# A two-branch kernel (spectral filter and softmax attention) whose instruction order is planned with a lock between GpSimd and VectorE

## The chip, the cores and the metric

The kernel runs on one core of a Trainium2 chip. A core has five engines with queues of their own: TensorE (PE; PEld is its weight load), VectorE (DVE), ScalarE (ACT), GpSimd (POOL) and SyncE (SP), which issues most DMAs. Each engine takes its instructions strictly in the order of its queue and waits on semaphores where one needs another engine's result. The metric is the device time of one execution in microseconds (us); less is better. In the rows below, arena is the one large on-chip buffer and ps the eight banks of the accumulator memory.

## The reference

Two independent branches are computed and laid side by side in the output, 640 columns each:

```python
def _A_ref(x, w_r, w_i):            # x: (1, 2048, 640)
    X = rfft2(x.astype(float32))    # over both axes
    X = X * (w_r + 1j * w_i)
    return irfft2(X, s=(2048, 640)).astype(bfloat16)

def _B_ref(x, wqkv, wo):            # x: (1, 2048, 640), 32 heads of 20
    qkv = (x @ wqkv).reshape(1, 2048, 3, 32, 20).transpose(2, 0, 3, 1, 4)
    q, k, v = qkv[0], qkv[1], qkv[2]
    p = softmax(einsum("bhqd,bhkd->bhqk", q, k) * 20 ** -0.5)
    o = einsum("bhqk,bhkd->bhqd", p, v)
    return o.transpose(0, 2, 1, 3).reshape(1, 2048, 640) @ wo

out = concatenate([_A_ref(...), _B_ref(...)], axis=-1)
```

## The kernel before

**Branch B, attention.** x is transposed on TensorE (job `xT`, L598), multiplied by the weights into keys and queries (jobs `p01` for keys and `p00` for queries of the first head groups, L620; `pk` for the others, L649) and into values (job `V`, L698). The first weights have to be copied apart first (`padw`, a VectorE copy, L559). A unit of work is four heads times 512 queries; there are 32 units of 64 score tiles of 128 keys by 512 queries, 2048 tiles in all. A tile's scores are one matmul (L817). Its exponential is taken in one of two ways:

- on ScalarE, two tiles in one instruction (`exp`, L1444, 128x1024);
- on VectorE, four tiles as a batch: the score is clipped into 16-bit integers (`p1`, L972, from ps), and two further 16-bit passes over 128x2048 elements in the arena make two more terms (`p2` L1020 and `p3` L1019). A batch multiplies the values three times, so it needs three times the matmuls L1102 of a ScalarE tile, and a scaled copy of the values (`vs`: GpSimd L1029, or VectorE L1031 early on).

TensorE multiplies values by the exponentials (`pv`, L1102); at the end of a unit the sum goes out of ps (L1133), its reciprocal takes a round trip through DRAM, and GpSimd scales the result (`onorm`, L1154). Job `OP` (L1248 and L1253) is the last projection, evicted at L1259 and stored.

**Branch A, the filter.** GpSimd folds x by its symmetries (`fold`, L1659 to L1666); jobs S1 (L1772), S2 (L1855), S3 (L1959) and S4 (L2011) are matmuls by tables with VectorE work behind each (S2: L1887 and L1895 to L1904; S4: a copy L2019 for a first half, and two L2030 for a second half). S4 is 32 jobs of six matmuls, four jobs for each of eight row blocks; a block is stored when its four jobs are done, and the second half of block n waits until block n-2 has been stored.

**What sets the order.** No order is written by hand. While the kernel is built, the class `KB` plays the whole program through with a clock of its own (`now`, and `free[engine]` for when each engine is done). At each step `step_pe` takes for TensorE, in this order: scores for ScalarE if two banks are free, multiplications by values, background jobs (`try_bg`, by priority `prio`, and only if the time left until ScalarE needs scores again has room for them), scores for VectorE (`try_dve_fill`). `pick_dve` takes for VectorE the ready instruction with the lowest priority number, and `pick_dve_tile` with `dve_wants` decides from VectorE's planned backlog how many tiles VectorE gets; ScalarE gets the rest. `put` books an instruction with an assumed duration and moves the planned clocks. So a changed duration or rule in the planner changes nothing that is computed, but can change every queue's order and the split of the 2048 tiles. On the chip the instructions then follow the queues and the semaphores.

Before, `put` knew one interaction between GpSimd and VectorE: a `p2` or `p3` that begins while GpSimd is busy was booked as longer by 0.44 of the overlap.

## Time and profile before

| | before |
|---|---|
| timed runs, us | 756.99, 756.69, 755.43 (median 756.69) |
| span of the profiled execution, us | 759.9 |
| that execution outside its span | no time of its own is given beside the span |
| ScalarE busy, us | 723.8 (95%), of it 774 exponentials 716.6 |
| TensorE busy, us | 722.7 (95%) |
| VectorE busy, us | 678.2 (89%) |
| GpSimd busy, us | 206.7 (27%) |
| granted TensorE clock, mean | 0.994 |

Busy shares are averages over the whole program. Matmuls are pipelined, and a matmul's record is longer than the time until the next can start, so TensorE's 95% is not a limit by itself; idle time before an instruction, and what ended it, says who waited for whom.

### The profile page before, as it was taken

How to read it: one execution, taken by the hardware profiler on the slowest of the kernel's cores; microseconds unless marked ns; L12 is line 12 of the kernel's file. 1: busy time of each engine (PE TensorE's matmuls, PEld its weight loads, DVE VectorE, ACT ScalarE, POOL GpSimd, SP SyncE). 2: the span in 40 equal slices, each digit the busy share in tenths (PEclk: the TensorE clock that was granted, in tenths of full speed). 3: DMA queues.
4: the chain of work that ended last, by engine and by line, in shares of the span. 5: the costliest groups of instructions: out<-in, count | busy, mean ns of one | idle time of the engine just before them, and what ended most of it. 6: DMA issues, size and time to landing. Idle time of an engine off the chain costs nothing.

```text
span 759.9 us, 16458 instructions
## 1 busy us (share of the span) xinstructions
PE 722.7 (95%) x6520; PEld 232.3 (31%) x6565; DVE 678.2 (89%) x1172; ACT 723.8 (95%) x787; POOL 206.7 (27%) x253
## 2 busy tenths in 40 slices
PE   8998999999999999999999999999999999999997
PEld 4422232332322222232223323322222232333333
DVE  3599999989989899999989988999899999999895
ACT  5899999999999999999999989999999999999994
POOL 7296952111211022122331123212121222122110
PEclk9999999999999999999999989999999999999999
DMA  9023321202102116213120112103010012111101
GB/s 314 11 72 90 96 71 52 48 20 49 34 21 57 42 46 222 76 37 104 38 53 16 47 37 51 24 21 110 20 44 22 16 46 84 38 45 48 51 23 56
DMA packets 43503, 44.68 MB, mean 59 GB/s; under 512 B 16740, under 2 KB 36582, under 8 KB 43166
## 3 DMA queue, kind: packets, MB, share of 16 engines
q1 hardware_dynamic: 42654, 42.25, 18.9%
q0 software_dynamic: 768, 1.32, 0.7%
q8 instruction: 54, 0.88, 0.5%
q14 instruction: 27, 0.22, 0.1%
HBM read 28.47 MB, written 8.36 MB: 48 GB/s over the span
## 4 chain that ended last, share of the span: by engine, by line
PE 51%; ACT 38%; DVE 9%; issue 2%; DVEq 0%
ACT arena L1444 37%; PE ps L817 18%; PE ps L1102 14%; PE ps L649 5%; DVE arena L972 3%; PE ps L698 3%; PE ps L1855 3%; PE ps L1772 2%; DVE arena L1019 2%; PE ps L1248 2%; PE ps L2011 2%; PE ps L1959 2%; DVE arena L1020 1%; PE ps L620 1%; PE ps L578 1%
## 5 line engine op out<-in xcount | busy, mean ns | idle before, releaser
L1444 ACT ACTIVATE arena<-ps 128x1024 f16<-128x1024 f32 x774 | 716.6, 1092 | 17.6 <-PE ps L817 11.2
L972 DVE TENSOR_SCALAR arena<-ps 128x512 int16<-128x512 f32 (+1 forms) x490 | 330.8, 692 | 31.8 <-PE ps L817 30.4
L817 PE MATMUL ps<-arena 32*128 32x512 bf16 x2048 | 304.9, 386 | 13.6 <-ACT arena L1444 10.0
L1102 PE MATMUL ps<-arena 128*32 128x512 f16 x3048 | 240.9, 386 | 4.4 <-DVE arena L1019 2.1
L817 PEld LDWEIGHTS ps<-arena 32*128 32x128 bf16 x2048 | 75.1, 91 | 285.9 <-ACT arena L1444 255.9
L1029 POOL TENSOR_SCALAR arena<-arena 128x96 bf16<-128x96 bf16 x112 | 74.5, 669 | 250.6 <-PE ps L1102 245.7
L1019 DVE TENSOR_SCALAR arena<-arena 128x2048 int16<-128x2048 int16 x125 | 93.7, 750 | 5.5 <-PE ps L1102 5.1
L1154 POOL TENSOR_TENSOR arena<-arena 128x512 bf16<-128x512 f32 x30 | 40.6, 1353 | 204.8 <-DMA arena<-rd 204.7
L1020 DVE TENSOR_SCALAR arena<-arena 128x2048 int16<-128x2048 int16 x125 | 92.9, 743 | 1.5
L1102 PEld LDWEIGHTS ps<-arena 128*32 128x32 bf16 x3048 | 52.3, 94 | 104.2 <-issue 70.2
L649 PE MATMUL ps<-arena 128*128 128x512 bf16 x149 | 45.7, 383 | 4.2 <-issue 2.4
L1855 PE MATMUL ps<-arena 128*128 128x322 bf16 (+1 forms) x198 | 39.2, 311 | 3.3 <-DVE arena L1904 1.8
L2011 PE MATMUL ps<-arena 128*128 128x320 bf16 (+1 forms) x192 | 35.7, 302 | 0.1
L698 PE MATMUL ps<-arena 128*128 128x160 bf16 x320 | 32.2, 234 | 1.0 <-DVE arena L972 1.0
L1887 DVE TENSOR_TENSOR arena<-ps,arena 128x644 bf16<-128x644 f32 (+1 forms) x34 | 27.9, 821 | 4.1 <-PE ps L1855 2.3
L1959 PE MATMUL ps<-arena 128*128 128x512 bf16 (+3 forms) x123 | 29.9, 333 | 1.3 <-issue 1.3
L1248 PE MATMUL ps<-arena 128*128 128x320 bf16 (+1 forms) x152 | 28.2, 302 | 0.2 <-DVE arena L1887 0.2
L1133 DVE COPY arena<-ps 128x512 f32<-128x512 f32 (+1 forms) x33 | 22.0, 669 | 5.9 <-PE ps L1102 5.6
L698 PEld LDWEIGHTS ps<-arena 128*128 128x128 bf16 x320 | 21.1, 98 | 14.7 <-issue 11.1
L661 DVE TENSOR_SCALAR arena<-ps 128x512 bf16<-128x512 f32 x34 | 23.1, 678 | 0.1
L1772 PE MATMUL ps<-arena 128*128 128x512 bf16 x72 | 21.7, 383 | 1.0 <-issue 0.8
L1855 PEld LDWEIGHTS ps<-arena 128*128 128x128 bf16 (+1 forms) x198 | 14.9, 98 | 21.6 <-issue 10.8
(83 smaller groups left out, 369.9 us busy)
## 6 DMA issues: line engine op xcount, KB each, us to landing
arena<-rd SPq DMA_DIRECT2D x120, 64.0 KB
out_dram<-arena SPq DMA_DIRECT2D x32, 160.0 KB
arena<-in_A_x_dram SPq DMA_DIRECT2D x16, 160.0 KB
xs<-arena SPq DMA_DIRECT2D x16, 160.0 KB
arena<-xs SPq DMA_DIRECT2D x4, 640.0 KB
arena<-arena SPq DMA_DIRECT2D x105, 20.0 KB
arena<-ct SPq DMA_DIRECT2D x2, 1024.0 KB
arena<-ct SPq DMA_DIRECT2D x4, 512.0 KB
```

The costliest lines, as they stand in the source:

```text
L649: return lambda e: e.matmul(o, l, r_, start=(cc == 0), stop=(cc == 4))
L698: return lambda e: e.matmul(o, l, r_, start=st, stop=(c == 4), skip_group_check=True)
L817: return e.matmul(self.ps[:, bank, :], self.KT[32 * j:32 * j + 32, g, kt * 128:(kt + 1) * 128], self.QT[32 * j:32 * j + 32, g, qc * 512:(q ...
L972: return e.tensor_scalar(o, in_, 0.0, 31744.0, ALU.max, ALU.min)
L1019: self.dve_push([(lambda e, en: e.tensor_scalar(Ii, Ii, SH2, 0.0, ALU.subtract, ALU.max), occ, ik + pk, ik, [], "p3")], lambda: push(self. ...
L1020: ops = [(lambda e, en: e.tensor_scalar(Gi, Ii, SH1, 0.0, ALU.subtract, ALU.max), occ, ik, [("G", b)], [], "p2")]
L1029: self.pool_op(lambda e: e.tensor_scalar(vs, vi, W1, None, ALU.mult), 300.0, r=vr, w=vk, name="vs")
L1102: inst = e.matmul(self.ps[32 * j:32 * j + 32, bank, :], v_, p_, start=s_, stop=False, tile_position=(0, 32 * j), skip_group_check=True)
L1444: self.put("act", lambda e: e.activation(o, in_, AF.Exp, bias=ACT_BIAS, scale=ACT_SCALE), 0.8333 * 512 * n + 60.0, r=[("ps", b) for b in b ...
L1855: return lambda e: e.matmul(o, lhs, r_, start=st, stop=sp)
L1959: return lambda bank: (lambda e: e.matmul(ps[0:M, bank, lo_:hi_], l, rhs, start=st, stop=sp, skip_group_check=True))
L2011: return lambda e: e.matmul(o, l, r_, start=(n == 0), stop=(n == 5))
```

## The change

The planner's model is changed in five ways; no instruction computes anything else than before.

- The lengthening by 0.44 of the overlap goes. In its place the names in `PORT` exclude one another between VectorE and GpSimd: such an instruction is booked to begin only when the other engine's last one of `PORT` is over (`plock`). `PORT` has the 16-bit passes `p2` and `p3`, `vs`, the weight copies `padw`, the second and later instructions of S2's eviction (renamed `S2.evL`), and nearly all that GpSimd does, its memsets too.
- `pick_dve` passes over an instruction of `PORT` while GpSimd's lock lasts more than 100 ns longer, and takes another one.
- The assumed times of GpSimd's work change (`onorm` 1600 to 1250 ns, `vs` 300 to 430, the folds).
- `p2` and `p3` are assumed 32 ns shorter for a batch, and `exp` 8 ns shorter.

```diff
+        self.plock = {"pool": 0.0, "dve": 0.0}
...
-        if eng == "dve" and name in ("p2", "p3", "p4") and self.free["pool"] > st:
-            occ += min(self.free["pool"] - st, 1.8 * occ) * 0.44
+        port = name in self.PORT
+        if port and eng == "dve":
+            st = max(st, self.plock["pool"])
+        if port and eng == "pool":
+            st = max(st, self.plock["dve"])
         end = st + occ
+        if port:
+            self.plock[eng] = end
...
+    PORT = {"p2", "p3", "vs", "S2.evL", "padw", "onorm", "fold", "ms_vp", "ms_v1", "ms_k", "ms_q", "x24z", "wpad", "wz", "ms_sb"}
...
-        occ = 100 + 0.26 * 512 * n
+        occ = 68 + 0.26 * 512 * n
...
-                ops.append((mk(J.bank), occ, [key] + list(rk), list(wk), list(pwk), J.name + ".ev"))
+                ops.append((mk(J.bank), occ, [key] + list(rk), list(wk), list(pwk), J.name + (".evL" if J.name == "S2" and ops else ".ev")))
...
             if self.P.peek(en, r=op[2], w=op[3], pw=op[4]) > self.now:
+                continue
+            if op[5] in self.PORT and self.plock["pool"] > self.now + 100.0:
                 continue
...
-        return 0.8333 * 512 * n + 60.0
+        return 0.8333 * 512 * n + 52.0
```

What this does to the queues is seen at three places. Lines of the changed kernel are 8 higher than those of before in branch B and 10 higher from L1444 on.

**The start.** TensorE's queue before, from its first matmul: 11 warm-up matmuls, 20 transposes, one filler, the first keys and queries (10 matmuls), 20 transposes, and then the first scores (L817).

```order
L578 MATMUL ps<-arena 128x512 x11
L598 MATMUL ps<-arena 128x128 x20
L1536 MATMUL ps<-arena 128x512
L620 MATMUL ps<-arena 128x512 x10
L598 MATMUL ps<-arena 128x128 x20
L817 MATMUL ps<-arena 128x512 x4
L698 MATMUL ps<-arena 128x160 x14
```

The same place in the changed kernel (scores are L825 now, the weight products L628).

```order
L586 MATMUL ps<-arena 128x512 x11
L606 MATMUL ps<-arena 128x128 x20
L628 MATMUL ps<-arena 128x512 x5
L606 MATMUL ps<-arena 128x128 x20
L628 MATMUL ps<-arena 128x512 x5
L706 MATMUL ps<-arena 128x160 x10
L628 MATMUL ps<-arena 128x512 x5
L606 MATMUL ps<-arena 128x128 x10
L825 MATMUL ps<-arena 128x512 x4
L706 MATMUL ps<-arena 128x160 x18
```

The first queries, which the first scores need, are now the third group of five, behind a second block of keys and ten value matmuls; the filler is gone. On VectorE, the four copies of weights (L559 before, L567 now) stood together at the head of the queue. In the changed kernel's VectorE queue they are spread:

```order
L567 COPY arena<-arena 128x20x20
L612 COPY arena<-ps 128x2x256 x2
L636 TENSOR_SCALAR arena<-ps,arena 128x512
L612 COPY arena<-ps 128x2x256
L612 COPY arena<-ps 128x3x256
L567 COPY arena<-arena 128x20x20
L636 TENSOR_SCALAR arena<-ps,arena 128x512
L567 COPY arena<-arena 128x20x20
L636 TENSOR_SCALAR arena<-ps,arena 128x512
```

The second copy, which the first queries need, stands behind four evictions of transposes (L612) and one of keys (L636).

**ScalarE.** The piece of the difference that holds its exponentials:

```order
-L604 COPY arena<-ps 128x3x256
-L604 COPY arena<-ps 128x2x256
-L604 COPY arena<-ps 128x3x256 x2
-L604 COPY arena<-ps 128x2x256
-L1444 ACTIVATE arena<-ps 128x1024 x774
+L612 COPY arena<-ps 128x3x256 x3
+L612 COPY arena<-ps 128x2x256
+L712 CAST arena<-ps 128x2x8x20
+L612 COPY arena<-ps 128x3x256
+L1454 ACTIVATE arena<-ps 128x1024 x780
```

Six exponentials more, so twelve tiles more are ScalarE's; VectorE has 122 batches in place of 125.

**The end.** TensorE's last rows of the main program before; the matmuls of S4 (L2011) ended among the scores, 32 rows ahead of the last one here.

```order
L1300 MATMUL ps<-arena 1x5
L1253 MATMUL ps<-arena 128x320 x3
L1248 MATMUL ps<-arena 128x320 x4
L1253 MATMUL ps<-arena 128x320 x3
L1248 MATMUL ps<-arena 128x320 x4
L1253 MATMUL ps<-arena 128x320 x2
L1248 MATMUL ps<-arena 128x320 x4
L1253 MATMUL ps<-arena 128x320 x2
```

And in the changed kernel, where S4 is L2021:

```order
L1308 MATMUL ps<-arena 1x5
L1261 MATMUL ps<-arena 128x320 x5
L1256 MATMUL ps<-arena 128x320 x4
L1261 MATMUL ps<-arena 128x320 x2
L1256 MATMUL ps<-arena 128x320 x4
L1261 MATMUL ps<-arena 128x320 x2
L2021 MATMUL ps<-arena 128x320 x66
```

Eleven of the 32 jobs of S4, 66 matmuls, now stand behind everything else; with them move 17 VectorE evictions and six stores of branch A to the end of their queues. From the last multiplication by values on, 33 matmuls of L1256 and L1261 follow, where 38 of L1248 and L1253 followed before.

## Rows read from the trace of the kernel before

**Rows 1.** Span and mean clock; the page: busy time and chain by engine.
```profile
core 0: 759.9 us, clock 0.994
...
PE 722.7 (95%) x6520; PEld 232.3 (31%) x6565; DVE 678.2 (89%) x1172; ACT 723.8 (95%) x787; POOL 206.7 (27%) x253
PE 51%; ACT 38%; DVE 9%; issue 2%; DVEq 0%
```
**Rows 2.** Groups by line: busy, mean ns, idle before and its releasers.
```profile
L1444 ACT ACTIVATE arena<-ps 128x1024 f16<-128x1024 f32 x774 | 716.6, 1092 | 17.6 <-PE ps L817 11.2 <-PE ps L1102 4.6
L2030 DVE TENSOR_TENSOR arena<-arena,ps 128x320 bf16<-128x320 f32 x32 | 15.2, 475 | 1.5 <-PE ps L2011 1.4
```
**Rows 3.** Timeline of ScalarE, first 40 us, and its last exponentials.
```profile
7.10 1.99 ACT L604 COPY arena<-ps 128x768 bf16<-128x768 bf16 x3 [4.88 <-PE ps L598]
11.93 1.37 ACT L604 COPY arena<-ps 128x768 bf16<-128x768 bf16 x2 [2.83 <-PE ps L598]
13.78 14.77 ACT L1444 ACTIVATE arena<-ps 128x1024 f16<-128x1024 f32 x16 [0.48 <-PE ps L817]
29.59 5.61 ACT L1444 ACTIVATE arena<-ps 128x1024 f16<-128x1024 f32 x6 [1.04 <-PE ps L817]
37.48 2.85 ACT L1444 ACTIVATE arena<-ps 128x1024 f16<-128x1024 f32 x3 [2.28 <-PE ps L817]
...
734.54 12.94 ACT L1444 ACTIVATE arena<-ps 128x1024 f16<-128x1024 f32 x14 [0.32 <-PE ps L1102]
```
**Rows 4.** The chain that ended last: start, us, what; its longest piece.
```profile
554.27 65.22 ACT arena L1444 x71
```
**Rows 5.** ScalarE's exponentials from 60 to 120 us.
```profile
L1444 ACT ACTIVATE arena<-ps 128x1024 f16<-128x1024 f32 x62 | 58.2, 1043 | 2.5 <-PE ps L817 2.0 <-PE ps L1102 0.3
```
**Rows 6.** One stretch: us, busy of PE, PEld, DVE, ACT, POOL; clock, DMA, GB/s.
```profile
440.00:460.00 20.00, 18.46 (x140) 5.47 (x133) 15.06 (x25) 16.20 (x18) 4.76 (x5) 0.83 0.13 35
```
**Rows 7.** Timeline of all engines, 6 to 14 us.
```profile
6.00 1.33 DVE L559 COPY arena<-arena 128x400 bf16<-128x400 bf16 x4 [3.13 <-DMA arena<-in_B_wqkv_dram]
6.37 0.95 POOL L570 MEMSET arena<- 128x1024 f32 x1
...
9.24 2.32 PE L620 MATMUL ps<-arena 128*128 128x512 bf16 x10 [0.40 <-ACT arena L604]
...
11.32 1.18 PEld L598 LDWEIGHTS ps<-arena 128*128 128x128 bf16 x20 [0.26 <-DVE arena L628]
11.59 0.75 DVE L628 TENSOR_SCALAR arena<-ps,arena 128x512 bf16<-128x512 f32 x1 [0.33 <-PE ps L620]
...
13.68 1.14 PE L698 MATMUL ps<-arena 128*128 128x160 bf16 x14
```
**Rows 8.** VectorE's 16-bit pass L1020: ns shortest, median, longest; and 32 to 104 us.
```profile
L1020 DVE TENSOR_SCALAR arena<-arena x125: 627/685/1943, 39.1 to 745.7; 128x2048 int16<-128x2048 int16 x125
L1020 DVE TENSOR_SCALAR arena<-arena 128x2048 int16<-128x2048 int16 x11 | 11.5, 1044 | 0.1
```
**Rows 9.** Timelines of GpSimd and VectorE about 88 us.
```profile
87.89 1.40 POOL L1659 TENSOR_TENSOR arena<-arena 128x640 f32<-128x640 bf16 x1
...
88.50 1.34 DVE L1020 TENSOR_SCALAR arena<-arena 128x2048 int16<-128x2048 int16 x1
```
**Rows 10.** Timeline of the end, 736 to 760 us.
```profile
736.86 0.86 PE L2011 MATMUL ps<-arena 128*128 128x320 bf16 x5
737.97 0.58 PE L2011 MATMUL ps<-arena 65*128 65x320 bf16 x3
...
754.79 0.44 PE L1253 MATMUL ps<-arena 80*128 80x320 bf16 x2
755.26 0.43 ACT L1259 CAST arena<-ps 128x320 bf16<-128x320 f32 x1 [1.22 <-PE ps L1253]
...
755.71 0.33 SPq L486 DMA_DIRECT2D out_dram<-arena  x1
```

More of the change, by code (lines that the diff above doesn't have):

```diff
@@ L1028, in close_batch @@
         if self.folded():
[L1029 removed]
+            self.pool_op(lambda e: e.tensor_scalar(vs, vi, W1, None, ALU.mult), 430.0, r=vr, w=vk, name="vs")
         else:
@@ L1153, in norm_dma @@
         pk = self.pack_keys(u - 1) if u else []
-        self.pool_op(lambda e: e.tensor_tensor(on, of, bc, ALU.mult), 1600.0, r=pk + [("bcu", u, j) for j in range(4)] + [("bc", j) for j in range(4)] + [("Of", b2)],
+        self.pool_op(lambda e: e.tensor_tensor(on, of, bc, ALU.mult), 1250.0, r=pk + [("bcu", u, j) for j in range(4)] + [("bc", j) for j in range(4)] + [("Of", b2)],
                      w=[("On",), ("Onu", u)] + al, name="onorm")
@@ L1443, in try_exp @@
         in_ = self.ps[:, banks[0]:banks[0] + n, :].rearrange("p b n -> p (b n)")
-        self.put("act", lambda e: e.activation(o, in_, AF.Exp, bias=ACT_BIAS, scale=ACT_SCALE), 0.8333 * 512 * n + 60.0,
+        self.put("act", lambda e: e.activation(o, in_, AF.Exp, bias=ACT_BIAS, scale=ACT_SCALE), 0.8333 * 512 * n + 52.0,
                  r=[("ps", b) for b in banks], w=keys, name="exp")
@@ L1658, in fold_x @@
             k = [("fxl", t, 0), ("fxl", t, 1), ("fx", f, 0), ("fx", f, 1), D1, ("z", "C", 0)]
-            self.pool_op((lambda xa, xb: lambda e: e.tensor_tensor(a_, xa, xb, ALU.add))(xa, xb), 1600.0, r=k, w=[("ft", 0), D0] if t == 0 else [("ft", 0)], name="fold")
-            self.pool_op((lambda xa, xb: lambda e: e.tensor_tensor(b_, xa, xb, ALU.subtract))(xa, xb), 1500.0, r=k, w=[("ft", 1), D0] if t == 0 else [("ft", 1)], name="fold")
+            self.pool_op((lambda xa, xb: lambda e: e.tensor_tensor(a_, xa, xb, ALU.add))(xa, xb), 1360.0, r=k, w=[("ft", 0), D0] if t == 0 else [("ft", 0)], name="fold")
+            self.pool_op((lambda xa, xb: lambda e: e.tensor_tensor(b_, xa, xb, ALU.subtract))(xa, xb), 1460.0, r=k, w=[("ft", 1), D0] if t == 0 else [("ft", 1)], name="fold")
             for i, (src, dst) in enumerate(((a_, xa), (b_, xb))):
@@ L1663, in fold_x @@
                 kk = [("ft", i), D1, ("z", "C", 0)]
[L1664 to L1666 removed]
+                self.pool_op((lambda d, s_: lambda e: e.tensor_copy(d, s_))(dst[:, 0:321:320], src[:, 0:321:320]), 275.0, r=kk, w=[("fx", f, i), ("ff", t, i, 0)], name="fold")
+                self.pool_op((lambda d, l, h: lambda e: e.tensor_tensor(d, l, h, ALU.add))(dst[:, 1:320], lo, hi), 820.0, r=kk + [("ff", t, i, 0)], w=[("ff", t, i, 1)], name="fold")
+                self.pool_op((lambda d, l, h: lambda e: e.tensor_tensor(d, l, h, ALU.subtract))(dst[:, 321:640], lo, hi), 815.0, r=kk + [("ff", t, i, 0)], w=[("ff", t, i, 2)], name="fold")
                 self.dma(self.xs[i][128 * t:128 * t + 128, :], dst, 163840, r=[("ff", t, i, q) for q in range(3)] + [("fx", f, i), ("z", "C", 0)], w=[("xs", i, t)], name="st_fx")
```

4 lines of the change are left out of this document (removed).

## The prediction

> **What bounds the kernel now.** I read the page first. TensorE and ScalarE are both busy for 95% of the span of 759.9 us, and the chain that ended last lies 51% on TensorE and 38% on ScalarE [rows 1], so the page alone does not say which of them sets the pace. The groups by line do: the 774 exponentials fill 716.6 us, 926 ns each (716.6 / 774; the mean of 1092 ns is longer because neighbours overlap in the records), and ScalarE sits idle before them for only 17.6 us [rows 2]. By the timeline of ScalarE the first begins at 13.78 us and the last piece ends at 734.54 + 12.94 = 747.5 us [rows 3]. So the span falls into three parts: 13.8 us until the first exponential, 733.7 us of exponentials with 17.1 us of idle time among them (the 17.6 without the 0.48 ahead of the first), and a tail of 12.4 us. For 65 us in one piece the chain runs over 71 exponentials with no gap, 919 ns each [rows 4]. I take the middle as paced by ScalarE, and ask of each edit what it does to the start, the count, the gaps and the tail.
>
> The gaps lie in four places. Two at the start are 1.04 and 2.28 us long, before the exponentials at 29.59 and 37.48 us [rows 3]. From 60 to 120 us, where GpSimd folds, there are 2.5 us [rows 5]. From 440 to 460 us ScalarE is busy for 16.20 us of 20, so 3.8 us are lost, and there the granted clock is 0.83, that is part of the stretch at the lower level [rows 6]. The rest, 17.1 - 3.3 - 2.5 - 3.8 = 7.5 us, is spread over 600 us.
>
> **The start.** Before, all four weight copies were done by 7.33 us, and the first scores stood behind 10 matmuls of L620 and 20 transposes [rows 7]. Now the first queries come third. I follow the new queues with the durations of the old. The evictions of the first 20 transposes on ScalarE are two of about 0.8 us from 7.10 us (with a third one the group ended at 9.09 us [rows 3]), so they end near 8.7, and the first keys run from 8.85 to 10.0 (five of ten matmuls in 2.32 us [rows 7]). The second 20 transposes take about 1.3 us (their loads 1.18 [rows 7]). Their data was there at 11.32 us, when they began behind a VectorE eviction [rows 7]; whether earlier, no row says, so they begin between 10.0 and 11.3. Two more ScalarE evictions (1.37 us [rows 3]) bring the second keys to 12.2 to 13.4; ten value matmuls at 0.07 us (14 in 1.14 us [rows 7]) lead to 14.05; the first queries end at 15.2; ten transposes follow; the queries' eviction of 0.75 us [rows 7] starts near 15.3 and ends at 16.05; scores and the wait of ScalarE for them, 0.5 us, put the first exponential at 16.6 us, or at 17.9 if the data comes at 11.3. That is 2.8 to 4.1 us later than 13.78; I take **+3.3**, with 2.4 as the lower end since ten transposes may overlap the eviction better. In return the two gaps of 3.3 us should go: before, TensorE's queue had 20 and 27 matmuls in one run between two scores there, and the new queue has none over 10 there after the 18 values behind the first scores: **-3.3** (0 to -3.3).
>
> [...] Rows first: each of the four weight copies took a quarter of 1.33 us while GpSimd's memsets of 0.95 us ran back to back [rows 7], so these two do not exclude one another, and the new order delays the copies for a lock that the chip does not have there. [...]
>
> **The count.** ScalarE gets 780 exponentials: 6 x 0.926 = **+5.6 us**. VectorE loses twelve tiles and three batches; that takes work off an engine that is idle for 80 us, so it is worth something only where ScalarE's gaps come from it.
>
> **The exclusion itself.** It is real for the 16-bit passes: their median is 685 ns, but 1044 ns in the mean from 32 to 104 us, and up to 1943 ns [rows 8]. One that began at 88.50 us beside a fold that ran to 89.29 ended 0.55 us after the fold [rows 9]. Over the eleven L1020 there this is 11 x (1044 - 685) = 3.9 us, about 7 for both passes. But VectorE's delay reaches the end only through ScalarE's gaps, 2.5 us in that stretch [rows 5]. A better order can win at most these; with less VectorE work there too I take **-1.5** (0 to -2.5).
>
> **The remaining gaps.** I leave the 7.5 us as they are (0 to -4 at the bounds). The 3.8 us of the lower clock I neither save nor lose: the median of the timed runs, 756.69 us, is 3.2 us below the profiled span, so they may not have it at all.
>
> **The tail.** This is the largest term. S4's 66 matmuls stand behind everything. Where five of them run in a row they take 0.86 us and three 0.58 us [rows 10], so 0.14 us each: 66 x 0.14 = 9.2 us, and nothing is left on ScalarE to hide them. Their 17 evictions are 17 x 0.475 = 8.1 us of VectorE [rows 2], which runs beside them. Behind the last matmul two such evictions stand where one of 0.43 us stood, and two stores where one was (0.33 us to issue [rows 10]): +0.7. Block 7's second half must wait for block 5's store: TensorE wants it some 3 us after block 5's last eviction (five jobs of 0.84 us, less the lag of the evictions), and the old tail bounds a store between nothing and 759.9 - 755.7 = 4.2 us, plus the second issue: 0 to 1.9 us, of which I take 0.5. Five matmuls fewer follow the last multiplication by values: -0.7. Together **+9.7** (8.5 to 11.8).
>
> **Sum.** 3.3 - 3.3 + 5.6 - 1.5 + 9.7 = +13.8 us. Against the profiled span this is 759.9 + 13.8 = 773.7 with its slow-clock stretch; against the median, which I predict for, 756.69 + 13.8 = 770.5 us, 1.8% slower.
>
> **Rivals.**
> - *The middle is not paced by ScalarE.* TensorE's 51% of the chain speaks for it: then less VectorE work and smoother blocks shorten the middle. The price is at most all 17.1 us of gaps and, from 926 down to the 919 ns of the gapless piece, 780 x 7 ns = 5.5 us: 756.7 + 3.3 + 5.6 + 9.7 - 22.6 = 752.7, faster. It decides only if gaps and slack together fall by over 17.1 us (18.6 less the 1.5 us that 0.2% of this time is, which is about what a measurement can tell from no change). The gapless 65 us speak against it. 4%.
> - *A dip that was there in the timed runs goes.* The order around 450 us is new; if the timed runs before did lose 3.8 us there, the new kernel ends at 766.7. Against it speaks the 3.2 us between median and span. 20%.
> - *The clock falls in a new place.* A stretch like that at 450 us costs 3.8 us: 774.3. If it is the 66 matmuls, which wait for evictions and a store, the half clock doubles them: 779.7. For it: after a gap in TensorE's work the clock did fall here once. Against: the mean clock of 0.994 [rows 1] leaves 0.6% of the time, 4.6 us, for lower clocks in all, and the stretch at 450 us alone is 3.4 us of that (20 x 0.17 [rows 6]), so the old tail, with waits of its own, had at most 1.2. 14%.
> - *The change does not do what it says.* The passes wait for GpSimd as before since the chip's timing drifts from the plan: the -1.5 and part of the -3.3 go, 774. It is inside the forecast's own range.
>
> **Chances and range.** The forecast has 62%, with 766 to 775 as its own range (the start, gaps and tail at half their bounds). The rivals have 4, 20 and 14. The range that holds 8 in 10 reaches from the vanished dip with slightly smaller gaps, 764, to a new dip with all upper ends, 778. Faster needs the first rival whole: 2%. Within 0.2% needs most of it: 3%. Slower by more: 95%.
>
> **What would show it.** Right: the exponentials begin near 17 us and are 780 at 926 ns; gaps among them below 13 us with none over 1 us before 60 us; at the end one run of 66 S4 matmuls, some 9 to 10 us long, behind the last L1261, with ScalarE idle; the tail behind the last exponential near 22 us. The passes' mean may fall below 750 ns with no gain. Wrong: the last exponential ends well before 745 us, or the 66 matmuls take under 7 or over 13 us, or a new stretch at the lower clock.

## The result, and the profile after

The changed kernel takes 763.02 us (median of 8 runs, 762.26 to 764.16) against 756.81 us for the kernel before in the same comparison (8 runs, 755.43 to 760.5): a ratio of 1.0082, with 95% from 1.0064 to 1.0099. It is slower by 6.2 us, as forecast in sign, but 770.5 us had been forecast and 764 was the lower end.

The profiled execution took 763.24 us, 1.84 of them outside its span. First the page: span, busy time by engine, and the chain that ended last.

```profile
span 761.4 us, 16376 instructions
PE 726.1 (95%) x6497; PEld 235.4 (31%) x6545; DVE 667.1 (88%) x1133; ACT 726.6 (95%) x794; POOL 202.6 (27%) x254
ACT 76%; PE 18%; DVE 4%; issue 1%
```

The shares of the engines are within a point of [rows 1]. The chain is not: 76% ScalarE where it was 38%. The groups by line show what changed (busy, mean ns, idle before and its releasers):

```profile
L1454 ACT ACTIVATE arena<-ps 128x1024 f16<-128x1024 f32 x780 | 718.6, 1118 | 5.8 <-PE ps L825 2.6 <-PE ps L1110 2.4
L2040 DVE TENSOR_TENSOR arena<-arena,ps 128x320 bf16<-128x320 f32 x32 | 15.3, 478 | 2.5 <-PE ps L2021 1.9
```

There are 780 exponentials as forecast, but they take 718.6 / 780 = 921 ns each instead of 926, and ScalarE is idle before them for 5.8 us instead of 17.6 [rows 2]. ScalarE's timeline, its start and its last exponentials:

```profile
15.68 0.80 ACT L612 COPY arena<-ps 128x768 bf16<-128x768 bf16 x1 [0.99 <-PE ps L606]
16.58 24.86 ACT L1454 ACTIVATE arena<-ps 128x1024 f16<-128x1024 f32 x27
41.75 8.41 ACT L1454 ACTIVATE arena<-ps 128x1024 f16<-128x1024 f32 x9 [0.32 <-PE ps L825]
50.73 1.02 ACT L1454 ACTIVATE arena<-ps 128x1024 f16<-128x1024 f32 x1 [0.56 <-PE ps L825]
52.23 4.69 ACT L1454 ACTIVATE arena<-ps 128x1024 f16<-128x1024 f32 x5 [0.48 <-PE ps L825]
57.72 2.85 ACT L1454 ACTIVATE arena<-ps 128x1024 f16<-128x1024 f32 x3 [0.80 <-PE ps L825]
...
712.16 28.69 ACT L1454 ACTIVATE arena<-ps 128x1024 f16<-128x1024 f32 x31
```

The first exponential begins at 16.58 us (13.78 in [rows 3]) and the last ends at 712.16 + 28.69 = 740.85 (747.48). The two stalls of 1.04 and 2.28 us (a stall is a gap of over 1 us) are gone. So the three parts of the span are 16.6, 724.3 and 20.5 us, after 13.8, 733.7 and 12.4: start +2.8, middle -9.4, tail +8.1. Of the middle's 9.4 us, 3.8 are the stretch at the lower clock [rows 6]; a second profile of the unchanged kernel, told of below, has none at that place. The median can't have had it whole: it has a span of 756.8 - 1.84 = 755.0, and the profiled execution without the stretch would have 756.1. (So the profiled span lies 4.9 us above the median's, not the 3.2 that the prediction took by setting a span beside a time.) Against a typical execution of before, an estimate from that span of 755.0 and the start and tail of 13.5 and 12.7 that two profiles show, so with a middle near 728.8, the middle is 4.5 us shorter. The forecast had it 0.8 longer.

The start in detail, from the timeline of all engines:

```profile
8.79 1.24 PE L628 MATMUL ps<-arena 128*128 128x512 bf16 x5 [0.84 <-ACT arena L612]
9.86 0.72 PE L606 MATMUL ps<-arena 128*128 128x128 bf16 x10
10.87 0.73 PE L606 MATMUL ps<-arena 128*128 128x128 bf16 x10 [0.29 <-DVE arena L636]
...
11.69 0.96 POOL L578 MEMSET arena<- 128x1024 f32 x1
11.89 0.35 DVE L567 COPY arena<-arena 128x400 bf16<-128x400 bf16 x1
...
13.37 0.85 PE L706 MATMUL ps<-arena 128*128 128x160 bf16 x10
...
14.06 1.24 PE L628 MATMUL ps<-arena 128*128 128x512 bf16 x5
15.14 0.72 PE L606 MATMUL ps<-arena 128*128 128x128 bf16 x10
...
16.15 0.40 PE L825 MATMUL ps<-arena 32*128 32x512 bf16 x4 [0.29 <-DVE arena L636]
```

Keys at 8.79, the second transposes from 9.86 (the early end of what I allowed), values at 13.37, queries at 14.06, scores at 16.15: the chain I had followed through the queue. A weight copy of 0.35 us lies inside a memset of 0.96 us, so the copies do not wait for GpSimd in this kernel either. And the end, from the timeline of TensorE, VectorE and SyncE:

```profile
746.99 0.44 PE L1261 MATMUL ps<-arena 80*128 80x320 bf16 x2
747.26 9.16 PE L2021 MATMUL ps<-arena 128*128 128x320 bf16 x66
...
755.64 2.05 DVE L2040 TENSOR_TENSOR arena<-arena,ps 128x320 bf16<-128x320 f32 x4 [0.33 <-PE ps L2021]
757.20 1.30 SPq L494 DMA_DIRECT2D out_dram<-arena  x2
```

One run of 66 matmuls in 9.16 us, 0.139 each; the forecast's 9.2. The difference to the forecast is therefore mostly in the middle, and the experiments go after it.

### The profile page after: what moved, and what is told of

The parts are those of the page before. It is cut to its first block, busy times and chain, and to the rows that moved or that the text cites. A ratio compares the mean times of both kernels' runs of the same rounds, so it can differ in the third digit from the quotient of the medians.

```text
span 761.4 us, 16376 instructions
## 1 busy us (share of the span) xinstructions
PE 726.1 (95%) x6497; PEld 235.4 (31%) x6545; DVE 667.1 (88%) x1133; ACT 726.6 (95%) x794; POOL 202.6 (27%) x254
## 4 chain that ended last, share of the span: by engine, by line
ACT 76%; PE 18%; DVE 4%; issue 1%
ACT arena L1454 76%; PE ps L825 6%; PE ps L1110 4%; PE ps L2021 2%; PE ps L657 2%; DVE arena L980 1%; PE ps L628 1%; PE ps L1256 1%; DVE arena L1027 1%; DVE arena L1028 1%; PE ps L706 1%; PE ps L586 1%; PE ps L1969 0%; DVE arena L636 0%; PE ps L1782 0%
## 5 line engine op out<-in xcount | busy, mean ns | idle before, releaser
L1454 ACT ACTIVATE arena<-ps 128x1024 f16<-128x1024 f32 x780 | 718.6, 1118 | 5.8 <-PE ps L825 2.6
L980 DVE TENSOR_SCALAR arena<-ps 128x512 int16<-128x512 f32 (+1 forms) x462 | 321.3, 711 | 40.3 <-PE ps L825 37.8
L825 PE MATMUL ps<-arena 32*128 32x512 bf16 x2048 | 306.9, 384 | 17.7 <-ACT arena L1454 11.3
L825 PEld LDWEIGHTS ps<-arena 32*128 32x128 bf16 x2048 | 75.8, 91 | 286.9 <-ACT arena L1454 265.3
L1027 DVE TENSOR_SCALAR arena<-arena 128x2048 int16<-128x2048 int16 x122 | 90.9, 748 | 2.7 <-PE ps L1110 2.0
L1028 DVE TENSOR_SCALAR arena<-arena 128x2048 int16<-128x2048 int16 x122 | 88.0, 721 | 1.4
L657 PE MATMUL ps<-arena 128*128 128x512 bf16 x149 | 45.7, 383 | 2.6 <-issue 2.3
L2021 PE MATMUL ps<-arena 128*128 128x320 bf16 (+1 forms) x192 | 33.3, 301 | 0.2 <-DVE arena L980 0.2
L1256 PE MATMUL ps<-arena 128*128 128x320 bf16 (+1 forms) x152 | 28.9, 302 | 0.0
L712 DVE CAST arena<-ps 128x320 bf16<-128x320 f32 x31 | 15.2, 489 | 9.4 <-PE ps L706 9.3
```

What stands on the lines that cost most here:

```text
L657: return lambda e: e.matmul(o, l, r_, start=(cc == 0), stop=(cc == 4))
L825: return e.matmul(self.ps[:, bank, :], self.KT[32 * j:32 * j + 32, g, kt * 128:(kt + 1) * 128], self.QT[32 * j:32 * j + 32, g, qc * 512:(q ...
L980: return e.tensor_scalar(o, in_, 0.0, 31744.0, ALU.max, ALU.min)
L1027: self.dve_push([(lambda e, en: e.tensor_scalar(Ii, Ii, SH2, 0.0, ALU.subtract, ALU.max), occ, ik + pk, ik, [], "p3")], lambda: push(self. ...
L1028: ops = [(lambda e, en: e.tensor_scalar(Gi, Ii, SH1, 0.0, ALU.subtract, ALU.max), occ, ik, [("G", b)], [], "p2")]
L1454: self.put("act", lambda e: e.activation(o, in_, AF.Exp, bias=ACT_BIAS, scale=ACT_SCALE), 0.8333 * 512 * n + 52.0, r=[("ps", b) for b in b ...
```

## The experiments

For each kernel I read the start, the middle (first exponential to the end of the last), its stalls (gaps of ScalarE over 1 us) and the tail from the profiled execution. Where I count **waits of the middle**, they are its length, less the stalls, less 0.919 us for each exponential. 0.919 is the pace without gaps [rows 4]; the changed kernel has it too, by the longest piece of its chain (start, us, what):

```profile
428.85 153.45 ACT arena L1454 x167
```

153.45 / 167 is 0.919. Waits hold the small gaps and what each gap costs besides: an exponential that runs alone takes 1.02 us (the row at 50.73 above) and three in a row 2.85, so a run is some 0.1 us longer than its count times 0.919, and each interruption adds that once. They also hold what a stretch at the lower clock costs beyond stalls (3.8 us in that of [rows 6]). Three names stand in the first expectations. ROOM: the exponential planned 8 ns shorter leaves less room for background work on TensorE between two scores, so gaps close, and S4 is left over for the tail. MOVED: the 66 matmuls of S4 that left the middle relieved it. LOCK: the better model of the exclusion closed the gaps.

### The tail alone

Two kernels leave out the last eleven S4 jobs (66 matmuls, 17 evictions, six stores), so part of the filter's output isn't written; the rest of the order stays.

```diff
+        for eng, pre, n in (("pe", "S4.pe", 66), ("dve", "S4.ev", 17), ("sp", "st_A", 6)):
+            gone.update([t for t in P.order[eng] if t.name.startswith(pre)][-n:])
```

**After without them** (after_drop):

> The changed kernel without the same eleven S4 jobs, which are its tail (that part of the filter's output is left out). Every theory: the tail falls from 20.5 to about 12.4 us, and the time by 8.1 us to 754.9 (754 to 756). If it falls by less, something other than the 66 matmuls also ends late.

754.33 us, ratio to before 0.9962 (0.9943 to 0.998). That is 8.7 us less than the whole changed kernel, and the middle is the same: the tail costs 8.7 us and nothing else hangs on it.

**Before without the same jobs** (before_drop):

> The kernel before with its queues kept, but without the last eleven S4 jobs (66 matmuls, 17 VectorE evictions, 6 stores; that part of the filter's output is left out). Theory ROOM (the planner's shorter exponential leaves less room for background work between two scores, so ScalarE's small gaps go all over the middle and the work left over lands in the tail): the jobs lie where ScalarE has no gaps, so little changes: 755.5 to 757 us. Theory MOVED (the middle of the changed kernel is shorter because these jobs no longer load TensorE and VectorE there): most of the 4.5 us come off: 751 to 753 us.

764.15 us, ratio 1.01 (1.0076 to 1.0124): with less work it is slower. The windows of its last 60 us (PE, PEld, DVE, ACT, POOL busy; granted clock, DMA share, GB/s):

```profile
680.00:700.00 20.00, 19.49 (x187) 6.30 (x185) 18.03 (x35) 20.00 (x23) 4.21 (x5) 1.00 0.15 45
700.00:708.00 8.00, 6.91 (x64) 1.71 (x64) 7.07 (x13) 7.92 (x9) 1.37 (x2) 0.88 0.13 43
708.00:716.00 8.00, 7.31 (x49) 1.27 (x46) 4.87 (x9) 6.99 (x8) 0.00 (x0) 0.50 0.15 35
716.00:724.00 8.00, 6.10 (x60) 1.48 (x58) 5.07 (x8) 7.99 (x10) 2.13 (x3) 0.93 0.04 12
724.00:732.00 8.00, 8.00 (x50) 2.92 (x46) 4.59 (x8) 6.04 (x7) 0.95 (x1) 0.50 0.01 2
```

Where the S4 matmuls are missing, TensorE is busy for 6.91 of 8 us from 700 us (7.93 in the kernel before, at a clock of 1.00), and the granted clock falls to 0.50 of full speed; in the two windows at 0.50 ScalarE is busy for 6.99 and 6.04 of 8 us, after 7.92. So S4 had also kept TensorE occupied there, and the run can't tell ROOM from MOVED. What speaks against MOVED is a place: the gaps closed between 120 and 600 us, where both kernels have no S4 yet (it begins near the 660th exponential before, the 695th after): ScalarE is idle there for 1.9 us after, and for 7.7 in the second profile of before.

### The parts of the change

**The lock and the passing over alone** (excl_only): all assumed durations as before. The edit is against the changed kernel, and the lines of GpSimd's durations are left out.

```diff
-        occ = 68 + 0.26 * 512 * n
+        occ = 100 + 0.26 * 512 * n
...
-        return 0.8333 * 512 * n + 52.0
+        return 0.8333 * 512 * n + 60.0
```

> The lock between GpSimd and VectorE and the skipping in the planner, with all assumed durations as before (exponential 60 ns over its rate); 774 exponentials, late first queries, no S4 in the tail. ROOM: the gaps in the middle are those of before, so 756.8 + 2.8 for the start = 759.5 us (758 to 761), ScalarE idle 12 us or more. Theory LOCK (the better model of the exclusion is what closed the gaps): 756.8 + 2.8 - 8 = 752 us (750 to 754), ScalarE idle under 8 us.

771.73 us, ratio 1.0185 (1.0162 to 1.0209), against all expectations. Timelines of ScalarE and of TensorE:

```profile
90.12 5.60 ACT L1454 ACTIVATE arena<-ps 128x1024 f16<-128x1024 f32 x6 [13.05 <-PE ps L1110]
```

```profile
78.64 5.70 PE L706 MATMUL ps<-arena 128*128 128x160 bf16 x80
84.18 4.48 PE L657 MATMUL ps<-arena 128*128 128x512 bf16 x20
88.59 1.48 PE L1110 MATMUL ps<-arena 128*32 128x512 f16 x24
```

The planner let 80 value matmuls and 20 for keys and queries (L657) run between two scores, and ScalarE stood still for 13.05 us. Why it did is not shown; my reading of the planner is that its VectorE passes did not get past the booked lock and that, by its own clock, ScalarE could not go on. Without that stall and one of 3.24 us at 52 us the waits are 16.3 us. This profile too has a stretch at the lower clock:

```profile
420.00:435.00 15.00, 13.81 (x96) 3.73 (x95) 10.94 (x19) 12.26 (x14) 3.46 (x6) 0.77 0.10 25
```

ScalarE lost 2.7 us there. Without them the waits are 13.6, beside 15.3 in the profile of before without the 3.8 of [rows 6]: the lock alone closes at most a small part of the gaps, far from LOCK's, and it brings the late start (16.58 us).

**The shorter exponential alone** (exp52), two numbers in the kernel before:

```diff
-        return 0.8333 * 512 * n + 60.0
+        return 0.8333 * 512 * n + 52.0
```

> The kernel before with one edit, the exponential planned 8 ns shorter; no lock. 776 exponentials, the old start, 48 S4 matmuls in the tail. ROOM: small gaps close although nothing of the lock is there: 13.8 + 776 x 0.921 + 8 + 12.4 + 48 x 0.14 + 1.8 = 757.4 us (756 to 759), ScalarE idle under 10 us. LOCK: 13.8 + 776 x 0.926 + 13.3 + 19.1 + 1.8 = 766.6 us (765 to 768), ScalarE idle 13 us or more.

763.74 us, ratio 1.006 (1.0035 to 1.0084). 776 exponentials, 48 S4 matmuls behind the last (6.71 us), waits 11.1 us; the time lies between the two theories. This one number makes most of the longer tail by itself, and part of the fewer waits.

**The whole change with the exponential back at 60** (after_exp60), the same edit the other way:

> The changed kernel, but the exponential planned 8 ns longer again (60 over its rate); lock, skipping and the other durations as in the change. 776 exponentials, late first queries, no S4 in the tail. ROOM (the shorter planned exponential is what closed ScalarE's gaps and pushed S4 out): the gaps of before come back, 776 x 0.926 + 10 to 13 us idle, so 16.6 + 718.6 + 12 + 12.4 + 1.8 = 761.4 us (759 to 763). LOCK (lock and shares closed them): 16.6 + 776 x 0.921 + 6 + 12.4 + 1.8 = 751.5 us (750 to 754).

766.52 us, ratio 1.0092 (1.006 to 1.0123). Slower than either theory. No S4 in the tail, as ROOM wants, but a stall of 8.01 us at 48 us, where TensorE runs 15 matmuls of L628, ten of L657 and 28 by values between two scores, and waits of 12.7 us.

**The lock without weight copies and memsets** (after_nopad), and the same with the exponential at 66 (nopad_exp66):

```diff
-    PORT = {"p2", "p3", "vs", "S2.evL", "padw", "onorm", "fold", "ms_vp", "ms_v1", "ms_k", "ms_q", "x24z", "wpad", "wz", "ms_sb"}
+    PORT = {"p2", "p3", "vs", "S2.evL", "onorm", "fold", "x24z", "wpad", "wz", "ms_sb"}
```

> The changed kernel, but with the weight copies and the set-up memsets not in the lock; the planner then gives the old start, 778 exponentials and no S4 in the tail. ROOM: the exponential is still planned 8 ns shorter, so the middle is tight: 13.8 + 778 x 0.921 + 5 + 12.4 + 1.8 = 749.6 us (748 to 752). MOVED: S4 is back among the scores and the gaps return: 13.8 + 778 x 0.926 + 12 + 12.4 + 1.8 = 760 us. If the start moves alone: 763.0 - 2.8 = 760.

> Lock without the weight copies and set-up memsets, exponential planned 66 ns over its rate: old start, 778 exponentials, no S4 in the tail, light VectorE load while GpSimd folds (0.75 us planned for each exponential). ROOM: the gaps are those of before or wider: 13.8 + 778 x 0.926 + 13 + 12.4 + 1.8 = 761.4 us. LOCK: 13.8 + 778 x 0.921 + 8 + 12.4 + 1.8 = 752.5 us.

758.89 us, ratio 1.0032 (1.0014 to 1.0051), and 758.46 us, ratio 0.9984 (0.9954 to 1.0015). Both start at the old time (13.31 and 13.82 us): taking these names out of the lock gives the start back. Both have the two old stalls; the first has one of 4.27 us besides and waits of 9.0, the second none and waits of 11.4. The first lands near what MOVED forecast in time (760), with fewer waits than it allows; the second lies between its two numbers. Neither leaves S4 for the tail, and neither beats the kernel before.

**Without the passing over** (noskip):

```diff
-            if op[5] in self.PORT and self.plock["pool"] > self.now + 100.0:
-                continue
```

> The changed kernel without the two lines of pick_dve that pass over an instruction whose lock is taken; the lock and the new durations (exponential planned at 52 over its columns) stay. Its queue has the old start (40 transposes and 4 keep-alives ahead of the first scores), 778 exponentials, three runs of TensorE work of 2.3, 3.0 and 3.3 us between two scores at the 17th, 23rd and 36th exponential, and 24 S4 matmuls behind the last one. If the late start belongs to the skip, the first exponential is at 13.1 to 13.8 us again. ROOM (the shorter planned exponential closes the small gaps, with the skip or without): 778 x 929 ns = 722.7, stalls 1.2 + 2.3 + 2.4, start 13.4, tail 12.4 + 24 x 0.132 = 15.6, in all 757.6 of span and 759.4 us of time. LOCK (the skip is what closed the gaps): 778 x 939 ns = 730.5, in all 767 us.

762.52 us, ratio 1.0044 (1.0018 to 1.007), between the two. The first exponential is at 13.65 us: the late start comes from passing over, not from the lock as booked. Beside the two old stalls there is one of 3.94 us before 51.6 us, and the mean clock of the first 60 us is 0.94; waits 10.7.

**The mild lock without passing over, exponential at 66** (nopad_noskip_exp66):

> The changed kernel with the lock kept for VectorE's 16-bit folds alone (weight copies and memsets out of it), without the passing over, and the exponential planned at 66: 778 exponentials, the old start, one run of 3.0 us at the 23rd, no S4 behind the last. It asks if the lock in this mild form beats the kernel before. If the middle per exponential is that of the kernel with the same set and the passing over (936 ns without its stalls): 778 x 0.936 = 728.2 + 2.3 + 13.5 + 12.4 = 756.4 of span, 758.3 us, level with before. If the lock does close gaps at this length too (930 ns): 753.6 us, faster by 0.4%. ROOM says the first, since the long planned exponential leaves the room; LOCK the second.

764.13 us in the median of the nine executions with a mean clock of 0.988 or more (765.83 with the three at 0.977 and 0.978), ratio 1.0082 (1.0047 to 1.0117), neither number. No other kernel here had executions so far apart in their mean clock (0.998 at 761.01, 0.977 at 775.71 us); its profile, at 759.2 us of span, has waits of 10.2 and, beside the old ones, a stall of 3.34 us at 46.5 us, with a mean clock of 0.97 in the first 60 us.

**The numbers alone** (const_only: the kernel before with all the new durations, no lock, no passing over), **and without the exponential's** (const_noexp):

> The kernel before with the change's numbers alone: the new durations of GpSimd's folds, multiplications and copies and of VectorE's passes, and the exponential planned at 52; without the lock and the passing over. 772 exponentials, the old start, runs of 2.3 and 3.0 us at the 17th and 23rd, 72 S4 matmuls behind the last exponential. I count the waits of the middle as its length, less stalls over 1 us, less 0.919 us (the pace of the piece without gaps) for each exponential: 15.3 and 16.1 us in the two executions of the kernel before, 11.1 with the exponential of 52 alone, 16.3 with the lock and the passing over alone, 7.5 with the whole change. NUMBERS (the new durations spread TensorE's work better and the lock has no part in it): 7.5 us of waits, so 772 x 0.919 = 709.5 + 7.5 + stalls 3.4 = 720.4, start 13.4, tail 12.4 + 72 x 0.132 = 21.9: 755.7 of span, 757.5 us. BOTH (the lock has its part once the numbers are right): 11 us of waits, 761 us.

> The same without the exponential's new length (60 as before): only the durations of GpSimd's work and of VectorE's passes are new. 770 exponentials, old start, one run of 3.0 us at the 23rd, 42 S4 matmuls behind the last. NUMBERS: the waits of the middle fall from 16 us to some 12.5 (the whole change at 60 has 12.7): 770 x 0.919 = 707.6 + 12.5 + 3.3 = 723.4, start 13.4, tail 12.4 + 5.5 = 17.9: 754.7 of span, 756.6 us. BOTH: 16 us of waits as in the kernel before, 760 us.

763.66 us, ratio 1.0092 (1.0063 to 1.0121), waits 11.5 us: BOTH by the waits, though slower than its 761. And 759.03 us, ratio 1.0027 (1.0006 to 1.0048), waits 12.7: NUMBERS by the waits, nearer to BOTH by the time. They contradict one another, so the fewer waits do not split into parts that add up.

### The margin, ROOM's own knob

One number of the kernel before, the margin that background work keeps to the next scores (445), up (before_fill461) and down (before_fill429):

```diff
-    FILL = 445.0
+    FILL = 461.0
```

> The kernel before with one number changed: the margin that TensorE's background work must keep to the next scores is 461 instead of 445, so 16 ns less room at the same planned exponential (60). 775 exponentials, one run of 3.0 us at the 23rd, 18 S4 matmuls behind the last. ROOM (what decides is how much background work the planner lets between two scores): the small gaps close as they did with the exponential of 52, some 930 to 934 ns per exponential: 775 x 932 ns = 722.3 + 2.3 + start 13.3 + tail 12.4 + 2.4 = 752.7 of span, 754.5 us. The rival (the gaps follow from the planned length of the exponential as such, through where VectorE's and GpSimd's work is placed, and not from the margin): 939 ns as before, 775 x 939 = 727.7, in all 758.1 of span, 760 us.

> The kernel before with the same margin at 429 instead of 445: 16 ns more room. 777 exponentials, one run of 3.0 us at the 23rd, no S4 behind the last. ROOM: the small gaps grow, some 945 ns per exponential: 777 x 945 = 734.3 + 2.3 + 13.3 + 12.4 = 762.3 of span, 764 us. The rival (margin without effect): 777 x 939 = 729.6, in all 757.6 of span, 759.4 us.

761.53 us (ratio 1.0028, 1.0006 to 1.005) with waits of 15.8, and 758.09 us (0.9973, 0.9947 to 0.9999) with waits of 11.9. (Two of the exponentials of each are of half size and counted as one.) More margin closed no gap, less margin opened none. ROOM, as a matter of how much room there is, falls. The second is level with the kernel before to slightly faster.

### What each engine costs in the middle

These add work of one engine to an order that stays as it is.

Ahead of every tenth score for VectorE, 41 in all, TensorE multiplies once more (before_more_pe):

```diff
+            if more:
+                e.matmul(self.ps[:, bank, :].rearrange("p (o n) -> p o n", o=4), self.ident, i4, start=True, stop=True)
+            return self.score_mm(e, u, kt, j, bank)
```

> The kernel before, its order untouched; ahead of every tenth score for VectorE (41 of them, over the whole middle) TensorE multiplies the identity once more by 512 columns into the same PSUM bank, which the score then overwrites: 41 x 0.216 = 8.9 us more of TensorE and nothing else. SCALAR: hidden beside the exponentials, 0 to 2 us slower, 757 to 759. SHARED with TensorE as the other pace: 6 to 9 us slower, 763 to 766.

775.46 us, ratio 1.0229 (1.0183 to 1.0275), more than either theory: 17 us for 41 matmuls, some 0.42 us each. The page and the groups:

```profile
PE 747.7 (97%) x6606; PEld 238.6 (31%) x6606; DVE 679.9 (88%) x1172; ACT 729.1 (94%) x787; POOL 208.1 (27%) x253
L1452 ACT ACTIVATE arena<-ps 128x1024 f16<-128x1024 f32 x774 | 721.9, 1055 | 25.8 <-PE ps L817 18.9 <-PE ps L1110 3.8 <-issue 0.4
L817 PE MATMUL ps<-arena 32*128 32x512 bf16 x2048 | 318.6, 384 | 9.5 <-ACT arena L1452 7.5 <-ACT arena L604 0.7 <-DVE arena L980 0.3
L964 PE MATMUL ps<-arena 128*128 128x512 bf16 x41 | 16.0, 389 | 0.0
```

ScalarE's gaps grew from 17.6 to 25.8 us [rows 2], and its exponentials from 926 to 933 ns each: more interruptions show in both. The scores use 32 of 128 rows, and four of them took 0.40 us together at 16.15 us above, where the record of one is 0.384. That a matmul over all rows among them ends this, and so costs more than its columns, is my reading, an estimate from these 0.42 us beside the 0.232 of each of ten matmuls over all rows that followed one another [rows 7]; no run separates it from the score's wait for the same bank.

Every sixth exponential, 109 in all, is split, in the kernel before (before_more_act) and in the changed one (after_more_act):

```diff
+            if more:
+                e.activation(o[:, 0:512], in_[:, 0:512], AF.Exp, bias=ACT_BIAS, scale=ACT_SCALE)
+                return e.activation(o[:, 512:1024], in_[:, 512:1024], AF.Exp, bias=ACT_BIAS, scale=ACT_SCALE)
```

> The kernel before, its order untouched; every sixth of the exponentials 61 to 719 (about 110) is issued as two halves of 128x512 instead of one of 128x1024. The work is the same; each split costs ScalarE one more instruction's fixed part, 926 - 853 = some 70 ns by the groups (853 ns is what 1024 columns take at 0.833 ns, the rate with which the program plans), so some 8 us of ScalarE's time in all, more than the six exponentials of the change (5.6 us). SCALAR (the middle of the kernel before is paced by ScalarE, the count term of the prediction was right, and something else closed the gaps): slower by 7 to 8 us, 764 to 765. SHARED (the middle lasts as long as TensorE or VectorE need, and ScalarE's gaps take up what it is given; over eight orders with 774 to 780 exponentials the middle without its long stalls was 724 to 728 us and did not grow with the count): slower by under 3 us, 757 to 760.

> The changed kernel with the same splitting of every sixth exponential, some 110, 8 us of ScalarE's time. Its ScalarE is idle for only 5.8 us in all. SCALAR: slower by 8 us than the changed kernel, 771. SHARED: the first 3 to 5 us are taken up by the gaps, 766 to 768.

765.8 us, ratio 1.0091 (1.0061 to 1.0121), and 769.15 us, ratio to before 1.0138 (1.0093 to 1.0183). Pages of the first and of the second:

```profile
PE 735.1 (96%) x6565; PEld 233.3 (31%) x6565; DVE 676.9 (89%) x1172; ACT 729.8 (95%) x896; POOL 206.0 (27%) x253
```

```profile
PE 736.9 (96%) x6545; PEld 235.5 (31%) x6545; DVE 667.9 (87%) x1133; ACT 732.7 (95%) x903; POOL 202.8 (26%) x254
```

ScalarE's busy time grew by 6.0 us (723.8 to 729.8) and by 6.1 (726.6 to 732.7), less than the 8 expected: in the first 55 ns for a split (6.0 / 109), where the expectation had some 70 from the planner's 853 ns; the time grew by 7.0 and by 6.1, the latter against the 763.02 of the first comparison (by the two ratios to before it is 4.2). SCALAR, in both, with its 8 us put at 6: what ScalarE is given lands on the time one to one within the noise of some 2 us, in the kernel with 17 us of gaps too.

Every second eviction of scores, 207 in all, is split (before_more_dve):

```diff
+            if more:
+                h = 256 * len(banks)
+                e.tensor_scalar(o[:, 0:h], in_[:, 0:h], 0.0, 31744.0, ALU.max, ALU.min)
+                return e.tensor_scalar(o[:, h:], in_[:, h:], 0.0, 31744.0, ALU.max, ALU.min)
```

> The kernel before, its order untouched; every second of VectorE's evictions of scores numbered 41 to 459 (about 210) is issued as two halves. Each split costs VectorE one more instruction's fixed part, some 70 ns (two of 512 columns, 681 ns each, against 1220 to 1225 for one of 1024), 15 us in all. SCALAR: hidden, 0 to 2 us slower, 757 to 759. SHARED with VectorE as the other pace: 8 to 15 us slower, 765 to 772.

758.54 us, ratio 0.9997 (0.997 to 1.0024). The page:

```profile
PE 726.9 (96%) x6565; PEld 232.2 (31%) x6565; DVE 690.4 (91%) x1379; ACT 724.1 (95%) x787; POOL 204.2 (27%) x253
```

12 us more of VectorE (678.2 in [rows 1]; 59 ns for a split) cost nothing that shows, within 2 us either way. The split evictions lie between 96 and 685 us, three of the 207 before 104 us. So the run doesn't price the 32 to 104 us in which the passes meet folds, about 7 us of loss in 72 [rows 8].

### The kernel before once more (before_again)

> The kernel before, unchanged, for a second profile. If the stretch at the lower clock near 450 us belongs to single executions, the span is near 755 to 756 us and ScalarE's idle time before exponentials near 13.5 us; if to the order, 760 and 17.6.

760.03 us, span 758.2; start 13.15, stalls of 1.04, 2.28 and 1.33 us, tail 12.95, waits 16.1. The span lies between the two that were expected. The granted clock is 1.00 in every window from 120 to 720 us, so the stretch of [rows 6] belongs to single executions. This one has a stretch of its own, with the third stall in it: from 72 to 80 us the clock is 0.79. Over all 122 timed executions of the kernel before that were run beside the experiments, the 33 with a mean clock of 1.000 have a median of 756.3 us, the 26 between 0.993 and 0.996 one of 760.0. The eight of the changed kernel all have 0.999 or 1.000.

### The waits side by side

From the profiled executions (stalls are the gaps over 1 us; more_act less its 6 us of added work). The third column from the right is the time in the middle at the lower clock, the next TensorE's idle time there that VectorE's instructions ended.

| | exponential planned | count | stalls, us | waits, us | lower clock, us | TensorE waits for VectorE, us | S4 matmuls behind |
|---|---|---|---|---|---|---|---|
| before | 60 | 774 | 3.3 | 19.1 (15.3 without the 3.8 of [rows 6]) | 6.8 | 10.2 | 0 |
| again; more_dve; more_act | 60 | 774 | 4.7; 4.7; 4.4 | 16.1; 17.6; 17.3 | 3.4; 3.4; 13.7 | 9.3; 11.7; 6.4 | 0 |
| excl_only | 60 | 774 | 16.3 | 16.3 | 6.8 | 5.5 | 0 |
| before_fill461 | 60 | 774 | 3.3 | 15.8 | 0 | 5.9 | 18 |
| after_exp60 | 60 | 776 | 11.1 | 12.7 | 3.4 | 8.6 | 0 |
| const_noexp | 60 | 770 | 5.4 | 12.7 | 0 | 4.9 | 42 |
| before_fill429 | 60 | 776 | 4.9 | 11.9 | 3.4 | 7.6 | 0 |
| const_only | 52 | 772 | 5.1 | 11.5 | 3.4 | 6.0 | 72 |
| exp52 | 52 | 776 | 4.9 | 11.1 | 0 | 6.0 | 48 |
| noskip | 52 | 778 | 7.4 | 10.7 | 6.8 | 3.7 | 24 |
| after_nopad | 52 | 778 | 7.7 | 9.0 | 0 | 2.3 | 0 |
| nopad_exp66 | 66 | 778 | 3.3 | 11.4 | 0 | 5.9 | 0 |
| nopad_noskip_exp66 | 66 | 778 | 8.3 | 10.2 | 3.4 | 4.2 | 0 |
| after; after_drop; after_more_act | 52 | 780 | 0 | 7.5; 7.3; 7.3 | 0 | 3.9; 2.9; 3.0 | 66; 0; 66 |

One order nearly keeps its waits (16.1 to 19.1 and 7.3 to 7.5 in repeats, the former with different times at the lower clock in them, the latter with none); another order has others, and every number moved makes another order. They are not fewer where more S4 was left over (11.5 with 72 matmuls, 9.0 with none), which MOVED would want. The kernel before lies near the top of the scatter, in part by the lower clock, and the changed one at its bottom. By and large, with exceptions such as excl_only and after_exp60, the waits go with the time that TensorE waits for VectorE.

## Why the prediction was right in sign and too high

- **Start, +3.3: right, 2.8.** The queue as followed; noskip and after_nopad show that it hangs on the names of the weight copies and memsets and on passing over.
- **The two stalls, -3.3: right.** Both are gone; four smaller gaps of 0.32 to 0.80 us that came at 41 to 58 us are in the waits.
- **Count, +5.6: right.** 6 x 0.919 = 5.5, and a price of one to one for ScalarE was measured in both orders, within the noise.
- **Exclusion, -1.5: not separated.** In the changed kernel the passes still meet folds (durations shortest, median, longest; then from 32 to 104 us):

```profile
L1028 DVE TENSOR_SCALAR arena<-arena x122: 628/684/1885, 41.6 to 736.0; 128x2048 int16<-128x2048 int16 x122
L1028 DVE TENSOR_SCALAR arena<-arena 128x2048 int16<-128x2048 int16 x9 | 8.3, 927 | 0.0
```

  927 ns instead of 1044 [rows 8], and still up to 1885: only a little shorter. But VectorE's delays also reach TensorE. Its multiplications by values and S2's matmuls, before and then after:

```profile
L1102 PE MATMUL ps<-arena 128*32 128x512 f16 x3048 | 240.9, 386 | 4.4 <-DVE arena L1019 2.1 <-DVE arena L1020 1.2 <-issue 0.5
L1855 PE MATMUL ps<-arena 128*128 128x322 bf16 x192 | 38.0, 311 | 3.3 <-DVE arena L1904 1.8 <-DVE arena L972 1.3 <-DVE arena L1887 0.2
```

```profile
L1110 PE MATMUL ps<-arena 128*32 128x512 f16 x3024 | 242.8, 386 | 1.4 <-DVE arena L1027 1.0 <-issue 0.3
L1865 PE MATMUL ps<-arena 128*128 128x322 bf16 x192 | 37.0, 304 | 0.2
```

  Over the middle TensorE's waits for VectorE fell from 10.2 us to 3.9, by about as much as ScalarE's waits. The prediction looked for VectorE's delays in ScalarE's gaps from 60 to 120 us alone. How much of this is the lock's is open: exp52 has 6.0 without the lock, after_exp60 8.6 with it.
- **The two rivals of the clock: neither came.** The mean clock after is 1.000, and the 66 matmuls took 0.139 us each at a granted clock of 1.00 (747.2 to 756.5 us). What they take at the lower clock no run shows; in the stretch of [rows 6] the clock was 0.50 from 451 to 457 us, and eight L1102 at 452.58 us took 1.04 us where eight at 457.53 took 0.62. The dip of [rows 6] was not in the median that I predicted for, which lies within 0.5 us of the 756.3 at full clock.
- **Tail, +9.7: mechanism right, 8.1 by the profiles and 8.7 by after_drop.** The 66 matmuls took the 9.2 us; what I had added for the store that block 7 waits for, and for the evictions behind, was too much together: the matmuls ran on with no gap.
- **The remaining gaps: the step that failed.** "I leave the 7.5 us as they are", with 926 ns taken as the price of an exponential. Against a typical execution of before the waits fell from some 14.2 us (728.8 - 3.3 - 774 x 0.919) to 7.5, by 6.7 where the exclusion and this step together had 1.5. These 5.2 us, 1.6 of the tail and 0.5 of the start are 7.3 of the 7.5 us between 770.5 and 763.0. The 14.2 is an estimate; the two profiles of before had 19.1 and 16.1, with 6.8 and 3.4 us at the lower clock.

That step held two mistakes. The 926 ns were no property of ScalarE: 7 ns of each, 5.3 us in all (716.6 - 774 x 0.919), were the 0.1 us that each interruption adds. ScalarE runs its exponentials in 58 uninterrupted pieces before and in 24 after, where 718.6 - 780 x 0.919 leaves 1.8 us. The gapless 919 of [rows 4] showed the difference, and I used it only for a rival. And I gave the gaps of the middle bounds of 0 to -4 as if the new order were the old one with edits. It is a new order of the middle too, and new orders made by small numbers had waits from 7.5 to 16.3 us.

The first rival, that the middle isn't paced by ScalarE, was half of the truth. It had the mechanism of the miss (gaps and slack that go) at 22.6 us and a chance of 4%; they were 6.7. By the prices both engines seem to pace the middle: ScalarE because each of its nanoseconds lands on the end, TensorE because a lump of 0.4 us ahead of a score does. Beside that, three batches fewer spare TensorE 24 matmuls by values (3048 to 3024), some 1.7 us by an estimate from the 0.55 us in which eight follow one another; I had counted them only as VectorE's. That part of the gain is argued, not shown.

**What stays open** is why this order has the fewest waits. Neither the lock (16.3 alone, 13.6 without its stretch at the lower clock), nor the shorter exponential (11.1), nor all the new numbers (11.5) reach 7.5; the margin moved nothing the way ROOM wants; const_only and const_noexp speak for different theories. The prices and TensorE's waits for VectorE, which are fewest in the orders with few waits, point to the order of TensorE's work, but no run changed those waits alone; which rule of the planner makes a good order isn't shown either. No kernel tried that writes the whole output beats the one before by more than 0.3% (before_fill429), with an interval that ends at 0.9999.

## What to carry to other kernels

When a planner's numbers change, price what the new order shows by itself (when the bottleneck's engine starts, how much it gets, what is left behind it), and give the stretch between a range as wide as different orders have there, not that of an edit. Take the price of an instruction from its gapless piece, since its mean over a busy program contains what each interruption adds (926 ns beside 919 here). Before a waiting engine is helped, add work to it in the unchanged order, and put the work where the engine is delayed: 12 us on VectorE cost nothing here, but nearly all of it lay outside the stretch that the lock was made for.

## What the hardware showed that I had not expected

- Leaving out 66 matmuls made the kernel before slower by 1%: the granted clock fell to 0.50 near 706 us. What came before was work of TensorE with short waits for ScalarE, the longest 0.53 us after 690 us:

```profile
703.67 0.39 PE L817 MATMUL ps<-arena 32*128 32x512 bf16 x2 [0.52 <-ACT arena L1444]
705.50 0.39 PE L817 MATMUL ps<-arena 32*128 32x512 bf16 x2 [0.53 <-ACT arena L1444]
```

- The same order is granted the lower clock in some executions and not in others, and at different places: near 450 us in one profile of the kernel before, near 75 us in the other. TensorE had just waited there for VectorE's L972, 1.26 and 0.78 us; what decides between executions stays open.
- One matmul over all 128 rows among scores of 32 rows cost some 0.42 us of time, though its 512 columns are planned at 0.216 and ten of that size in a row took 0.232 each [rows 7].
